# Two-bank score tiles, work placed at the ends of matmul groups, and an earlier load in a fused attention and MLP kernel

## The chip, the cores and the metric

The kernel runs on one core of a Trainium2 chip. The metric is the device time of one execution in microseconds (us). Before the change it was 414.0 us (median of three runs, 413.62 to 414.21). Runs of this kernel scatter by about 1%.

PE is the matmul engine, ACT evaluates activations, DVE is the vector engine, POOL the general-purpose engine, which here also issues the DMA transfers of the "software" queue; SP issues those of a "hardware" queue.

## The reference

```python
# q, k, v: (8, 12, 448, 64); w_in: (768, 2048); w_out: (2048, 768)
scores = q @ k.transpose(0, 1, 3, 2) / sqrt(64)
attn   = maximum(scores, 0) ** 2 / 448
x      = (attn @ v).transpose(0, 2, 1, 3).reshape(3584, 768)
h      = x @ w_in
out    = (maximum(h, 0) ** 2) @ w_out
```

The score part of one batch is three *units* of four heads, and each unit has seven *tiles*. There are 24 units (0 to 23) and 168 tiles in all.

## The kernel before

The program interleaves attention with the two large products. A *visit* computes two score tiles, takes the relu of them on ACT, does the product with v ("av", copied into xt, the transposed x) of two tiles of two visits ago, and squares the new tiles on DVE. Visits stand between the matmuls of h = x w_in (groups of six accumulating matmuls into one PSUM bank) and of the output product (groups of 16).

PSUM has eight banks: two for av, two for h and output ("mm"), four for a score tile pair ("s"). There is one such score slot.

```python
load16(n):  q, k of unit n as fp16, DMA from POOL with a cast (units 0 to 5; PE transposes them)
load_qk(n): q, k of unit n as fp32; cast_qk(n) casts them on POOL,
            dma_transpose(n) transposes them by DMA, issued from SP (units 6 to 23)

def scores(tiles):                      # cut to the part after the first stage
    at = at_p.tile([P, 4, S], FP16, name="at", tag="at")
    ps = slot(FP32)                     # four banks, one slot
    for z, t in enumerate(tiles):
        score(t, ps, z)
    nc.scalar.activation(out=at[:, 0:m], in_=ps[:, 0:m, 0:S], func=AF.Relu, scale=SK)

def enter_unit(n):                      # when the visits reach unit n
    m = n + 2
    if NPE + 2 <= m + 1 < NUN:
        load_qk(m + 1, nc.sync)
    if NPE <= m < NUN:                  # NPE = 6
        cast_qk(m)
        load_v(m)
        dma_transpose(m)

    ...                                 # loads issued from POOL, at the sixth visit
    load16(5); load_w1(3); load_v(5)
    for z in range(4):
        load_w2(z)                      # w_out, 768 KB each
    load_qk(6, nc.gpsimd)
    load_qk(7, nc.gpsimd)
    ...
    for cost, fn in steps:              # every h or output matmul is one step
        while ev and ev[0][0] <= clock: # visits may fall before any step
            ...
        fn()
        clock += cost
```

## Time and profile before

| | before |
|---|---|
| time, median | 414.0 us |
| span of the profiled run | 411.3 us |
| PE busy | 390.4 us (95%) |
| ACT busy | 233.3 us (57%) |
| DVE busy | 171.6 us (42%) |

These lines of the page give the busy time of each engine, and in 40 slices of the span the busy tenths of PE and the clock granted to it in tenths.

```profile
span 411.3 us, 7394 instructions
...
PE 390.4 (95%) x3188; PEld 196.9 (48%) x3188; DVE 171.6 (42%) x196; ACT 233.3 (57%) x283; POOL 79.4 (19%) x94
...
PE   6778996999999999999999999999999999999995
...
PEclk9999998999999999999999999999999999999999
```

PE is the limit nearly everywhere. What a reordering can win is its idle time, 20.9 us, and the time at a lowered clock. The view of waits names what ended PE's idle time: the waiting engine and line, the releaser, then the total in us, the count and the longest.

```profile
PE sps L213 <- DMA kT<-ks: 2.8, 1, 2.8
...
PE hps L321 <- ACT g L329: 1.9, 7, 0.4
...
PE hps L321 <- ACT at L230: 1.1, 1, 1.1
PE sps L213 <- DVE kT L184: 1.0, 2, 0.5
```

The largest single wait is for kT, the transposed k, of unit 6. The timeline of PE around it (start, duration, what, count, and in brackets the idle time before and its releaser):

```profile
63.08 0.93 PE L321 MATMUL hps<-xt,w 128*128 128x448 f16 x4
66.85 0.96 PE L213 MATMUL sps<-qT,kT 64*64 64x448 f16 x8 [2.85 <-DMA kT<-ks]
67.75 3.01 PE L321 MATMUL hps<-xt,w 128*128 128x448 f16 x9
71.01 1.67 PE L321 MATMUL hps<-xt,w 128*128 128x448 f16 x8 [0.25 <-ACT g L329]
```

Nine h matmuls took 3.01 us, where eight take 1.67 a little later: after the wait PE ran at half the clock (granted clock 0.50 from 66.7 to 70.1 us). The chain of waits, in order of time, leads from this wait back to the loads:

```profile
37.81 20.82 DMA qf<-in_q_dram
...
58.69 1.19 POOL qs L109
...
60.15 0.93 POOL ks L109
61.08 0.68 POOL vt L95
...
61.99 4.82 DMA kT<-ks
...
66.85 0.96 PE sps L213 x8
```

q of unit 6 was issued at 37.81 us, behind the four w_out loads of the same queue. Then came POOL's casts and the DMA transpose of k, which took 4.82 us from issue to landing.

### The profile page before, as it was taken

The page shows a single profiled execution, that of the slowest core. Times are in us where ns is not written, and L with a number is a line of the kernel's source. Part 1 is how long each engine was busy: PE and PEld are TensorE (multiplying, and loading weights), DVE is VectorE, ACT ScalarE, POOL GpSimd, SP SyncE. Part 2 cuts the span into 40 slices and gives each one's busy share as a digit, 9 for nine tenths or more (in the row PEclk, how much of TensorE's full clock was granted, in tenths as well). Part 3 has the DMA queues.
Part 4 walks back from the last instruction along what each step waited for, and adds up shares of the span by engine and source line. Part 5 has one row for each costly group of instructions (what it writes and reads, how often), then busy time and mean ns, then how long its engine had stood idle before and what let it go on. Part 6 is the DMA issues. An engine that isn't in the chain of part 4 may idle for free.

```text
span 411.3 us, 7394 instructions
## 1 busy us (share of the span) xinstructions
PE 390.4 (95%) x3188; PEld 196.9 (48%) x3188; DVE 171.6 (42%) x196; ACT 233.3 (57%) x283; POOL 79.4 (19%) x94
## 2 busy tenths in 40 slices
PE   6778996999999999999999999999999999999995
PEld 3333442445555544445555544444555544555663
DVE  1874674553343365563342356573332345220000
ACT  4976783774645567766544666765554575441111
POOL 8534124530020233030022033030000000000000
PEclk9999998999999999999999999999999999999999
DMA  8999999984566797352399776253251210001233
GB/s 126 202 201 206 210 260 204 276 167 81 163 109 164 144 233 163 59 121 47 79 194 209 171 178 156 37 134 55 48 115 47 70 40 0 2 0 40 77 78 77
DMA packets 62496, 50.81 MB, mean 124 GB/s; under 512 B 35712, under 2 KB 58688, under 8 KB 62464
## 3 DMA queue, kind: packets, MB, share of 16 engines
q1 hardware_dynamic: 46752, 33.86, 35.0%
q0 software_dynamic: 15552, 16.39, 24.2%
q8 instruction: 25, 0.41, 0.4%
q10 hardware_dynamic: 160, 0.10, 0.1%
q14 instruction: 7, 0.06, 0.0%
HBM read 45.61 MB, written 11.01 MB: 138 GB/s over the span
## 4 chain that ended last, share of the span: by engine, by line
PE 79%; DMA 14%; ACT 4%; POOL 2%; issue 1%; DVE 0%; POOLq 0%
PE ops L362 36%; PE hps L321 29%; PE sps L213 8%; PE avt L254 5%; DMA qf<-in_q_dram 5%; DMA w<-in_moe_w_in_dram 3%; ACT at L224 3%; DMA k<-in_k_dram 2%; DMA q<-in_q_dram 2%; DMA kT<-ks 1%; ACT g L329 1%; POOL vt L95 0%; POOL k L90 0%; POOL qs L109 0%; POOL q L89 0%
## 5 line engine op out<-in xcount | busy, mean ns | idle before, releaser
L321 PE MATMUL hps<-xt,w 128*128 128x448 f16 x768 | 156.7, 355 | 4.0 <-ACT g L329 1.9
L224 ACT ACTIVATE at<-sps 128x1792 f16<-128x1792 f32 x73 | 121.5, 1664 | 63.6 <-PE sps L213 63.4
L240 DVE TENSOR_TENSOR at<-at 128x1792 f16<-128x1792 f16 (+1 forms) x95 | 95.0, 1013 | 140.5 <-ACT at L224 137.5
L362 PE MATMUL ops<-w,g 128*128 128x384 f16 x896 | 152.0, 326 | 0.2 <-ACT g L329 0.2
L362 PEld LDWEIGHTS <-g 128*128 128x128 f16 x896 | 85.0, 98 | 66.1 <-issue 12.3
L321 PEld LDWEIGHTS <-w 128*128 128x128 f16 x768 | 71.6, 98 | 84.3 <-issue 24.3
L329 ACT ACTIVATE g<-hps 128x448 f16<-128x448 f32 x128 | 68.5, 543 | 49.8 <-PE hps L321 49.6
L332 DVE TENSOR_TENSOR g<-g 128x896 f16<-128x896 f16 x64 | 47.7, 746 | 32.0 <-ACT g L329 31.4
L384 ACT ACTIVATE osb<-ops 128x384 f32<-128x384 f32 x55 | 27.0, 490 | 49.5 <-PE ops L362 45.6
L109 POOL CAST qs<-qf 128x896 f16<-128x896 f32 x18 | 20.7, 1148 | 173.8 <-DMA qf<-in_q_dram 137.0
L254 PE MATMUL avt<-at,vt 64*64 64x448 f16 x672 | 46.9, 350 | 2.6 <-DVE xt L268 2.4
L213 PE MATMUL sps<-qT,kT 64*64 64x448 f16 x584 | 42.2, 364 | 5.0 <-DMA kT<-ks 2.8
L268 DVE TENSOR_SCALAR xt<-avt 128x896 f16<-128x896 f32 x23 | 25.0, 1087 | 18.8 <-PE avt L254 18.7
L213 PEld LDWEIGHTS <-kT 64*64 64x64 f16 x672 | 14.1, 105 | 35.9 <-issue 27.0
L254 PEld LDWEIGHTS <-vt 64*64 64x64 f16 x672 | 19.8, 107 | 16.0 <-issue 5.7
L109 POOL CAST ks<-kf 128x896 f16<-128x896 f32 x18 | 22.1, 1229 | 3.9 <-POOL qs L109 2.0
L230 ACT ACTIVATE at<-slot 128x896 f16<-128x896 f32 x22 | 18.5, 924 | 1.3 <-PE slot L213 1.1
L95 POOL DMA_DIRECT2D vt<-in_v_dram x24 | 17.3, 720 | 2.3 <-DMA w<-in_moe_w_in_dram 1.2
L378 DVE TENSOR_SCALAR osb<-ops 128x192 f32<-128x192 f32 x1 | 0.4, 358 | 35.6 <-ACT osb L375 35.6
L213 PE MATMUL slot<-qT,kT 64*64 64x448 f16 x88 | 7.2, 358 | 2.0 <-ACT kT L182 0.7
L132 POOL DMA_DIRECT2D w<-in_moe_w_in_dram x8 | 5.3, 666 | 3.4 <-DMA w<-in_moe_w_in_dram 1.2
L171 PE MATMUL slot<-zeros 128*128 128x448 f16 x12 | 4.6, 542 | 1.2 <-DVE zeros L147 1.2
(29 smaller groups left out, 40.7 us busy)
## 6 DMA issues: line engine op xcount, KB each, us to landing
out_dram<-osb SPq DMA_DIRECT2D x54, 192.0 KB, 2.7
qf<-in_q_dram SPq DMA_DIRECT2D x16, 448.0 KB, 5.0
kf<-in_k_dram SPq DMA_DIRECT2D x16, 448.0 KB, 5.6
vt<-in_v_dram POOLq DMA_DIRECT2D x24, 224.0 KB, 4.8
w<-in_moe_w_in_dram POOLq DMA_DIRECT2D x8, 384.0 KB, 11.7
w<-in_moe_w_out_dram POOLq DMA_DIRECT2D x4, 768.0 KB, 16.7
q<-in_q_dram POOLq DMA_DIRECT2D x6, 224.0 KB, 7.8
k<-in_k_dram POOLq DMA_DIRECT2D x6, 224.0 KB, 8.3
```

The costliest lines, as they stand in the source:

```text
L109: nc.gpsimd.tensor_copy(t.rearrange("p j h d -> p h j d"), src.rearrange("p h (j d) -> p h j d", d=D))
L213: nc.tensor.matmul(ps[c, 2 * z + hh, 0:S], lhsT=kT[r, j, c], rhs=qT[r, :, c], start=True, stop=True)
L224: nc.scalar.activation(out=at[:, 0:m], in_=ps[:, 0:m, 0:S], func=AF.Relu, scale=SK)
L230: nc.scalar.activation(out=at[:, 2 * z:2 * z + 2], in_=ps[:, :, 0:S], func=AF.Relu, scale=SK)
L240: nc.vector.tensor_mul(at[:, a:a + step], at[:, a:a + step], at[:, a:a + step])
L254: nc.tensor.matmul(ap[64 * hh:64 * hh + 64, hp, 0:S], lhsT=vt[r, hh, j * D:(j + 1) * D], rhs=at[r, hh, :], start=(j == 0), stop=(j == J - 1))
L268: nc.vector.tensor_scalar(out=xts[b][:, 2 * u:2 * u + 2, :], in0=ap[:, :, 0:S], scalar1=CX, scalar2=None, op0=ALU.mult)
L321: nc.tensor.matmul(cell[f][:, 0:S], lhsT=w1[f // 4][:, m, (f % 4) * P:(f % 4 + 1) * P], rhs=xts[b][:, m, :], start=(m == 0), stop=(m == NM ...
L329: nc.scalar.activation(out=g[:, f % 2], in_=cell[f][:, 0:S], func=AF.Relu)
L332: nc.vector.tensor_mul(g, g, g)
L362: nc.tensor.matmul(cell[0][:, 0:HALF], lhsT=gts[pr][f // 2][:, f % 2, tb * P:(tb + 1) * P], rhs=w2[f // 4][:, f % 4, hf * HALF:(hf + 1) * ...
L384: nc.scalar.activation(out=cell[1][:, z:z + HALF], in_=cell[0][:, 0:HALF], func=AF.Copy, scale=CO)
```

## The change

Its intent was to take these waits away:

- Score tiles of two PSUM banks in two slots, each with its own relu and square, instead of one slot of four banks.
- Among the h matmuls, visits and PE transposes only before the first matmul of a group (with one exception in batch 1); among the output matmuls they may stand anywhere, as before. The transposes of units 4 and 5 stand two groups ahead of their use.
- q and k of unit 6 are loaded ahead of w_out.
- In batch 0 every second h relu goes to DVE. The first h groups take the banks of a third score slot, which the first stage uses alone. The first visit to unit 6 comes eight h matmuls later than before.
- Smaller parts: v of unit 6 is loaded earlier, and the last copy of x for batch 1 is split between ACT and DVE, as that of batch 0 already was.

```diff
-    slot_p = first.enter_context(tc.tile_pool(name="slots", bufs=3, space=PSUM))
+    s_p = ctx.enter_context(tc.tile_pool(name="sps", bufs=2, space=PSUM))
+    third_p = first.enter_context(tc.tile_pool(name="third", bufs=1, space=PSUM))
 ...
+        ps = slot(FP32)                  # two banks, now inside score(t)
 ...
+        at = at_p.tile([P, 2, S], FP16, name="at", tag="at")
+        nc.scalar.activation(out=at, in_=ps[:, :, 0:S], func=AF.Relu, scale=SK)
 ...
+        for t in ready:
+            nc.vector.tensor_mul(ats[t], ats[t], ats[t])
 ...
+        return [(0.1892, step(m), m == 0 or (b == 1 and f == 0 and m == 4))
+                for m in range(NM)]
 ...
-            for z in range(4):
-                load_w2(z)
             load_qk(6, nc.gpsimd)
-            load_qk(7, nc.gpsimd)
+    load_v(6)
+    for z in range(4):
+        load_w2(z)
+    load_qk(7, nc.gpsimd)
 ...
-        while ev and ev[0][0] <= clock:
+        while ev and edge and ev[0][0] <= clock + 1e-3:
```

The number of matmuls, of visits and of transferred bytes stays the same.

More of the change, by code (lines that the diff above doesn't have):

```diff
@@ L63 @@
     v_p = ctx.enter_context(tc.tile_pool(name="vp", bufs=6))
-    at_p = ctx.enter_context(tc.tile_pool(name="atp", bufs=6))
+    at_p = ctx.enter_context(tc.tile_pool(name="atp", bufs=12))
     x_p = ctx.enter_context(tc.tile_pool(name="xp", bufs=3))
@@ L159 @@
     big: dict = {}
+    slot_no = [0]
     def slot(dtype):
-        if "s" in big:
-            return big["s"].tile([P, 4, 2048 // mybir.dt.size(dtype)], dtype,
-                                 name="sps", tag="s")
-        return slot_p.tile([P, 2, 2048 // mybir.dt.size(dtype)], dtype,
-                           name="slot", tag="slot")
+        slot_no[0] += 1
+        third = "mm" not in big and slot_no[0] % 3 == 2
+        return (third_p if third else s_p).tile(
+            [P, 2, 2048 // mybir.dt.size(dtype)], dtype, name="slot", tag="slot")
     def warm(n):
@@ L204, with score @@
     ats: dict = {}
-    def score(t, ps, z):
+    seen: dict = {}
+    now = [0]
+    av_order: deque = deque(range(NUN * J))
+    avt = [None]
+    def score(t):
         n, j = divmod(t, J)
         qT, kT = qkt[n]
+        ps = slot(FP32)
         for hh in range(2):
@@ L213, in score @@
                 nc.tensor.matmul(
-                    ps[c, 2 * z + hh, 0:S], lhsT=kT[r, j, c], rhs=qT[r, :, c],
+                    ps[c, hh, 0:S], lhsT=kT[r, j, c], rhs=qT[r, :, c],
                     start=True, stop=True)
-    def scores(tiles):
-        at = at_p.tile([P, 4, S], FP16, name="at", tag="at")
-        if "s" in big:
-            m = 2 * len(tiles)
-            ps = slot(FP32)
-            for z, t in enumerate(tiles):
-                score(t, ps, z)
-            nc.scalar.activation(
-                out=at[:, 0:m], in_=ps[:, 0:m, 0:S], func=AF.Relu, scale=SK)
-        else:
-            for z, t in enumerate(tiles):
-                ps = slot(FP32)
-                score(t, ps, 0)
-                nc.scalar.activation(
-                    out=at[:, 2 * z:2 * z + 2], in_=ps[:, :, 0:S], func=AF.Relu,
-                    scale=SK)
-        for z, t in enumerate(tiles):
-            ats[t] = at[:, 2 * z:2 * z + 2]
-        return at
-    def square(at, m):
-        step = 2 * m if "s" in big else 2
-        for a in range(0, 2 * m, step):
-            nc.vector.tensor_mul(at[:, a:a + step], at[:, a:a + step], at[:, a:a + step])
-    avt = [None]
+        at = at_p.tile([P, 2, S], FP16, name="at", tag="at")
+        nc.scalar.activation(out=at, in_=ps[:, :, 0:S], func=AF.Relu, scale=SK)
+        ats[t] = at
+        seen[t] = now[0]
     def av_round(t):
@@ L260, in av_round @@
                 xts[b] = x_p.tile([P, NM, S], FP16, name="xt", tag="xt")
-            if n == 2:
-                nc.scalar.activation(out=xts[b][:, 4, :], in_=ap[:, 0, 0:S],
+            xt = xts[b]
+            if b < 2 and u == NU - 1:
+                nc.scalar.activation(out=xt[:, 4, :], in_=ap[:, 0, 0:S],
                                      func=AF.Copy, scale=CX)
                 nc.vector.tensor_scalar(
-                    out=xts[b][:, 5, :], in0=ap[:, 1, 0:S],
+                    out=xt[:, 5, :], in0=ap[:, 1, 0:S],
                     scalar1=CX, scalar2=None, op0=ALU.mult)
@@ L268, in av_round, with av_some @@
                 nc.vector.tensor_scalar(
-                    out=xts[b][:, 2 * u:2 * u + 2, :], in0=ap[:, :, 0:S],
+                    out=xt[:, 2 * u:2 * u + 2, :], in0=ap[:, :, 0:S],
                     scalar1=CX, scalar2=None, op0=ALU.mult)
-    av_queue: deque = deque()
-    def av_some(upto, most):
+    def av_some(lag=2, most=3):
         done = 0
-        while av_queue and av_queue[0] <= upto and done < most:
-            t = av_queue.popleft()
+        while av_order and done < most:
+            t = av_order[0]
+            if t not in seen or seen[t] > now[0] - lag:
+                break
+            av_order.popleft()
             av_round(t)
@@ L281, in av_some, with prefetch, visit @@
                 break
-    seen = [0]
-    def enter_unit(n):
-        m = n + 2
+    def prefetch(m):
+        if m >= NUN:
+            return
         if NPE + 2 <= m + 1 < NUN:
             load_qk(m + 1, nc.sync)
-        if NPE <= m < NUN:
-            cast_qk(m)
+        cast_qk(m)
+        if m > NPE:
             load_v(m)
-            dma_transpose(m)
-    def visit(tiles, upto, most=3, turn=None):
+        dma_transpose(m)
+    def visit(tiles, turn=None, lag=2, most=3):
+        now[0] += 1
@@ L295, in visit @@
         for t in tiles:
-            if t % J == 0 and t >= 3 * J:
-                enter_unit(t // J)
-        at = scores(tiles) if tiles else None
+            if t % J == 0 and t >= (NPE - 2) * J:
+                prefetch(t // J + 2)
+        for t in tiles:
+            score(t)
         if turn is not None:
             pe_transpose(turn)
-        av_some(upto, most)
-        if tiles:
-            square(at, len(tiles))
-        av_queue.extend(tiles)
+        ready = list(tiles)
+        av_some(lag, most)
@@ L307, with h_group, step @@
+        for t in ready:
+            nc.vector.tensor_mul(ats[t], ats[t], ats[t])
     gts: dict = {}
-    def h_steps(b):
+    def h_group(b, f):
         pr = b // 2
-        if b % 2 == 0:
-            gts[pr] = []
         z = (b % 2) * S
-        steps = []
-        cell: dict = {}
-        def step(f, m):
+        cell = [None]
+        def step(m):
             def run():
                 if m == 0:
-                    cell[f] = big["mm"].tile([P, 512], FP32, name="hps", tag="mm")
+                    cell[0] = big["mm"].tile([P, 512], FP32, name="hps", tag="mm")
@@ L321, in run @@
                 nc.tensor.matmul(
-                    cell[f][:, 0:S],
+                    cell[0][:, 0:S],
                     lhsT=w1[f // 4][:, m, (f % 4) * P:(f % 4 + 1) * P],
                     rhs=xts[b][:, m, :], start=(m == 0), stop=(m == NM - 1))
-                if m == NM - 1:
-                    if b % 2 == 0 and f % 2 == 0:
-                        gts[pr].append(g_p.tile([P, 2, 2 * S], FP16, name="g", tag="g"))
-                    g = gts[pr][f // 2][:, :, z:z + S]
+                if m < NM - 1:
+                    return
@@ L329, in run @@
+                gs = gts.setdefault(pr, [])
+                if len(gs) <= f // 2:
+                    gs.append(g_p.tile([P, 2, 2 * S], FP16, name="g", tag="g"))
+                g = gs[f // 2][:, :, z:z + S]
+                if b == 0 and f % 2 == 1:
+                    nc.vector.tensor_scalar(
+                        out=g[:, f % 2], in0=cell[0][:, 0:S],
+                        scalar1=0.0, scalar2=None, op0=ALU.max)
+                else:
                     nc.scalar.activation(
-                        out=g[:, f % 2], in_=cell[f][:, 0:S], func=AF.Relu)
@@ L331, in run @@
-                    if f % 2 == 1:
-                        nc.vector.tensor_mul(g, g, g)
-            return run
-        order = [(f, m) for f in range(NF) for m in range(NM)]
-        if b < 2:
-            order.sort(key=lambda fm: (fm[0] // 2, fm[1] >= 4, fm)
-                       if fm[0] < 2 else (fm[0] // 2, 0, fm))
-        for f, m in order:
-            steps.append((0.1892, step(f, m)))
-        return steps
+                        out=g[:, f % 2], in_=cell[0][:, 0:S], func=AF.Relu)
@@ L343, in store @@
+                if f % 2 == 1:
+                    nc.vector.tensor_mul(g, g, g)
+            return run
+        return [(0.1892, step(m), m == 0 or (b == 1 and f == 0 and m == 4))
+                for m in range(NM)]
     def store(pr, tb, osb, c, eng):
@@ L395, in o_steps @@
                 for f in range(NF):
-                    steps.append((0.1625, step(tb, hf, f)))
+                    steps.append((0.1625, step(tb, hf, f), True))
         return steps
+    NB0 = NU * J
     warm(10)
     pe_transpose(0)
-    NB0 = NU * J
     for i in range(11):
-        visit([2 * i, 2 * i + 1], 2 * (i - 2) + 1, turn={1: 1, 4: 2, 7: 3}.get(i))
+        visit([2 * i, 2 * i + 1], turn={1: 1, 4: 2, 7: 3}.get(i))
         if i == 0:
@@ L417 @@
             load_v(5)
-            for z in range(4):
-                load_w2(z)
             load_qk(6, nc.gpsimd)
-            load_qk(7, nc.gpsimd)
+    load_v(6)
+    for z in range(4):
+        load_w2(z)
+    load_qk(7, nc.gpsimd)
     first.close()
-    for nm, n in (("mm", 2), ("s", 1)):
-        big[nm] = ctx.enter_context(tc.tile_pool(name=nm + "ps", bufs=n, space=PSUM))
-    events = []
-    T_H = NF * NM * 0.1892
+    big["mm"] = ctx.enter_context(tc.tile_pool(name="mmps", bufs=2, space=PSUM))
+    f0, f1 = h_group(0, 0), h_group(0, 1)
+    front = f0[0:4] + f1[0:4]
+    for _, fn, _ in front:
+        fn()
+    av_some(0, 9)
+    visit([NB0 + 1, NB0 + 2])
+    T_G = NM * 0.1892
+    T_H = NF * T_G
     T_O = NT_PAIR * 2 * NF * 0.1625
     T_P = 2 * T_H + T_O
-    seq = [11, 12, -4, 13, 14, 15, -5, 16, 17, 18, 19, 20]
-    events.append((1.5, [], NB0 - 1))
-    for z, i in enumerate(seq):
-        at = 2.0 + z * (T_H - 5.0) / 11
-        if i < 0:
-            events.append((at, None, -i))
-        else:
-            events.append((at, [2 * i, 2 * i + 1], 2 * (i - 2) + 1))
-    events.append((T_H - 1.6, [], 39))
-    events.append((T_H - 0.3, [], 41))
-    at0 = T_H + 0.5
-    for pr in range(1, 4):
+    events = []
+    seq = [[3, 4], 4, [5, 6], [7, 8], [9, 10], 5, [11, 12], [13, 14], [15, 16],
+           [17, 18], [19, 20], [], []]
+    for i, ts in enumerate(seq):
+        at = (2 + i) * T_G
+        if isinstance(ts, int):
+            events.append((at, lambda n=ts: pe_transpose(n)))
+        else:
+            events.append((at, lambda ts=ts: visit([NB0 + t for t in ts])))
+    events.append((T_H + 7 * 0.1892, lambda: av_some(0, 9)))
+    at0 = T_H + 2 * T_G
+    for pr in range(1, B // 2):
         t0 = 2 * NB0 * pr
@@ L447 @@
         for i in range(21):
-            t = t0 + 2 * i
-            events.append((at0 + i * gap, [t, t + 1], t - 3))
+            ts = [t0 + 2 * i, t0 + 2 * i + 1]
+            events.append((at0 + i * gap, lambda ts=ts: visit(ts)))
         at0 = end
     for i in range(3):
-        events.append((at0 + 0.3 + i, [], NUN * J))
-    steps = []
-    for pr in range(B // 2):
-        steps += h_steps(2 * pr) + h_steps(2 * pr + 1) + o_steps(pr)
-    clock = 0.0
-    ev = deque(events)
-    for cost, fn in steps:
-        while ev and ev[0][0] <= clock:
-            _, tiles, upto = ev.popleft()
-            if tiles is None:
-                pe_transpose(upto)
-            else:
-                visit(tiles, upto)
-        fn()
+        events.append((at0 + 0.3 + i, lambda: visit([])))
+    steps = [(0.1892, None, False)] * 8 + f0[4:] + f1[4:]
+    for f in range(2, NF):
+        steps += h_group(0, f)
+    f0, f1 = h_group(1, 0), h_group(1, 1)
+    steps += f0[0:4] + f1[0:4] + f0[4:] + f1[4:]
+    for f in range(2, NF):
+        steps += h_group(1, f)
+    steps += o_steps(0)
+    for pr in range(1, B // 2):
+        for b in (2 * pr, 2 * pr + 1):
+            for f in range(NF):
+                steps += h_group(b, f)
+        steps += o_steps(pr)
+    clock = 0.0
+    ev = deque(sorted(events, key=lambda e: e[0]))
+    for cost, fn, edge in steps:
+        while ev and edge and ev[0][0] <= clock + 1e-3:
+            ev.popleft()[1]()
+        if fn is not None:
+            fn()
         clock += cost
+    assert not ev and not av_order
 _INS = ['q', 'k', 'v', 'moe_w_in', 'moe_w_out']
```

## The prediction

> **What bounds it now.** The page's table of engines has PE busy 390.4 of 411.3 us; ACT is at 57%, DVE 42%, POOL 19%. So only PE's 20.9 us of idle time, and matmuls run at a lowered clock, can be won. The PE timeline and the PE waits place the idle time:
> - 0 to 27 us: about 6.9 us. Here ACT evacuates scores back to back (9.51 of 10 us busy in 10 to 20).
> - 27 to 62 us: 1.1 us (first h matmul waits for the last early relu, whose PSUM it takes over), 0.9 (xt of batch 0), 0.5 (score slot), 1.0 (kT copies after the transposes).
> - 64.0 to 66.85 us: 2.85 us for kT of unit 6. The chain of waits leads back to the load of its q, issued at 37.8 us behind four w_out loads and landed near 58. After this wait the windows show a granted clock of 0.50 (68 to 70 us); 9 h matmuls took 3.0 us instead of 1.7, a score visit 0.96 instead of 0.57: 1.7 us more. The Trainium skill, "TensorE: Matmul & The Clock Gate", section "What's actually happening", gives half the clock after an idle window of about 3.4 us, which fits.
> - 71 us on: about 1.9 us, eight waits of an h (or first out) matmul for its PSUM bank, whose relu stood behind a 1.66 us score relu.
> - The end: 4.4 us.
>
> **What the change does.**
> - Score relu: 73 of 128x1792 (1664 ns) become 146 of 128x896 (924 ns each; 846 apart back to back). That is 184 ns more per visit, 13 us of ACT busy time, as the skill's page "ScalarE: Activation LUTs", "What ACT_TABLE_LOAD costs", has it (186 ns + 0.833 per element; the trace agrees). Squares likewise: 2 x 548 for about 1010 ns. Neither engine bounds after 62 us, so this costs nothing there. In batch 0's h stage it is tight: per two visits about 4.0 us of ACT and 4.0 of DVE (odd relus go to DVE) against 4.3 of PE. I charge up to 1 us.
> - Two slots of two banks: transposes no longer take the only slot, and stand two groups ahead of use: minus 1.5 us.
> - h takes over the third slot's banks, free two relus earlier: minus 1 us; a score visit fills the xt wait: minus 0.5.
> - Visits at group edges: the preceding h relu is ahead of the score relus, so the bank is free in time: minus 1.5 us.
> - Unit 6 ahead of w_out: its q and k should land near 46 us, kT near 55. PE reaches it near 62. Minus 2.85 and 1.7 us.
> - Visits, matmuls and mode switches stay the same in number: PE work unchanged.
>
> Sum about -9.5 us, nearly all on PE, which is the critical path.
>
> **Prediction:** 404.5 us, range 401.5 to 408.5. Faster by over 2%: 0.66; within 2%: 0.32; slower: 0.02.
>
> **Right if:** PE idle falls to about 12 us; no wait for kT by DMA; granted clock near 1.00 from 60 to 70 us; PE's waits for the h relu nearly gone; ACT busy rises to about 240 us; the first out matmuls start near 83 to 84 us instead of 92. PE's time from there to the end shrinks by only about 1 us.
>
> **Wrong if:** unit 7's q and k, now last behind w_out and competing with unit 8's load (which starts earlier), land so late that kT of unit 7 (I estimate 71 us, needed near 75) stalls PE instead: up to 4 us back. Or ACT and DVE, both over 90% in batch 0's h stage, fall behind, so that av matmuls or h banks wait there: 1 to 3 us back. Or the early stage, bound by ACT, does not hand over sooner.

## The result, and the profile after

The changed kernel took 406.76 us (median of four runs, 406.32 to 408.73) against 413.81 us. The ratio was 0.9844, 95% interval 0.9805 to 0.9884: 1.6% faster, inside the predicted range, but not clear of 2%. A ratio here is always the mean time of one kernel's fast runs over that of the other's in the same rounds, so it is not quite the ratio of the medians.

```profile
span 404.6 us, 7633 instructions
...
PE 388.8 (96%) x3188; PEld 196.3 (49%) x3188; DVE 184.2 (46%) x277; ACT 233.9 (58%) x349; POOL 74.3 (18%) x94
...
PE   7689799999999999999999999999999999999995
...
PEclk9999899999999999999999999999999999999999
```

PE's idle time fell by 5.1 us to 15.8 us, not to 12. ACT's busy time did not rise to 240 us. The slow slice of PE and of its clock has moved forward, from about 60 to 70 us to about 40 to 50. PE's waits, changed kernel:

```profile
PE slot L219 <- DVE kT L185: 2.9, 2, 2.5
...
PE slot L219 <- DMA kT<-ks: 0.7, 1, 0.7
...
PE hps L304 <- ACT at L223: 0.3, 1, 0.3
```

The waits for the h relu are gone. The wait for kT of unit 6 is down to 0.7 us, but there is a new one of 2.5 us for a kT copy. PE's timeline, changed kernel:

```profile
44.23 0.38 PE L219 MATMUL slot<-qT,kT 64*64 64x448 f16 x4
47.16 0.59 PE L219 MATMUL slot<-qT,kT 64*64 64x448 f16 x4 [2.54 <-DVE kT L185]
47.53 0.96 PE L237 MATMUL avt<-at,vt 64*64 64x448 f16 x8
48.42 2.30 PE L304 MATMUL hps<-xt,w 128*128 128x448 f16 x6
...
61.60 4.83 PE L304 MATMUL hps<-xt,w 128*128 128x448 f16 x24
67.15 0.57 PE L219 MATMUL slot<-qT,kT 64*64 64x448 f16 x8 [0.72 <-DMA kT<-ks]
```

Six h matmuls took 2.30 us at 48.42; at full clock six take 1.31. And PE still cannot start unit 6 before 67.15 us (66.85 before). The chain of waits, changed kernel, says why:

```profile
42.96 3.09 DVE at L290 x2
...
46.16 20.94 DMA kT<-ks
...
67.15 0.57 PE slot L219 x8
```

The load of unit 6 came in early, the casts were done at 45.55 us, and the DMA transpose of k was issued at 46.16. But it took 20.94 us to land, where it took 4.82 before. It now ran beside the w_out loads.

The pair of squares at 42.96 us is slow too: two squares take 1.15 us elsewhere in this stage. These are lines of DVE and POOL from the timeline of all engines, changed kernel:

```profile
42.87 3.16 DVE L290 TENSOR_TENSOR at<-at 128x896 f16<-128x896 f16 x2
...
43.73 0.94 POOL L110 CAST qs<-qf 128x896 f16<-128x896 f32 x1
...
44.61 0.94 POOL L110 CAST ks<-kf 128x896 f16<-128x896 f32 x1
...
45.96 0.61 DVE L185 COPY qT<-slot 128x896 f16<-128x896 f16 x1
```

The first square took 0.62 us, the second 2.63; it ended only after both of POOL's casts. The Trainium skill, "SBUF — State Buffer", section "Who interferes with whom", says that a DVE instruction with two SBUF inputs contends with a POOL instruction that reads SBUF, and that whoever issues first makes the other wait. The amount fits: 2.0 us of delay against 1.82 us of casts. The order does not quite: the trace has the held square start 0.3 us before the first cast, and times on POOL are rough.

### The profile page after: what moved, and what is told of

It reads as the page before. It is cut to its first block, busy times and chain, and to the rows that moved or that the text cites. A ratio compares the mean times of both kernels' runs of the same rounds, so it can differ in the third digit from the quotient of the medians.

```text
span 404.6 us, 7633 instructions
## 1 busy us (share of the span) xinstructions
PE 388.8 (96%) x3188; PEld 196.3 (49%) x3188; DVE 184.2 (46%) x277; ACT 233.9 (58%) x349; POOL 74.3 (18%) x94
## 4 chain that ended last, share of the span: by engine, by line
PE 85%; DMA 7%; DVE 4%; ACT 2%; POOL 1%; issue 1%; SPq 0%; ACTq 0%; POOLq 0%
PE ops L347 37%; PE hps L304 33%; PE slot L219 8%; PE avt L237 6%; DMA kT<-ks 5%; DVE at L290 2%; DMA k<-in_k_dram 2%; ACT at L223 1%; DVE xt L252 1%; PE slot L192 1%; DVE qT L185 0%; POOL q L90 0%; DVE kT L185 0%; POOL k L91 0%; POOL vt L96 0%
## 5 line engine op out<-in xcount | busy, mean ns | idle before, releaser
L223 ACT ACTIVATE at<-slot 128x896 f16<-128x896 f32 x168 | 144.4, 918 | 47.3 <-PE slot L219 45.4
L304 PE MATMUL hps<-xt,w 128*128 128x448 f16 x768 | 155.0, 355 | 0.9 <-ACT at L223 0.3
L290 DVE TENSOR_TENSOR at<-at 128x896 f16<-128x896 f16 x168 | 108.7, 666 | 93.7 <-ACT at L223 93.7
L319 ACT ACTIVATE g<-hps 128x448 f16<-128x448 f32 x120 | 65.3, 545 | 55.0 <-PE hps L304 54.6
L322 DVE TENSOR_TENSOR g<-g 128x896 f16<-128x896 f16 x64 | 43.4, 679 | 52.6 <-ACT g L319 51.8
L219 PE MATMUL slot<-qT,kT 64*64 64x448 f16 x672 | 49.7, 362 | 5.2 <-DVE kT L185 2.9
L110 POOL CAST qs<-qf 128x896 f16<-128x896 f32 x18 | 19.2, 1064 | 168.3 <-DMA qf<-in_q_dram 142.4
L237 PEld LDWEIGHTS <-vt 64*64 64x64 f16 x672 | 19.6, 107 | 15.8 <-issue 5.9
L110 POOL CAST ks<-kf 128x896 f16<-128x896 f32 x18 | 18.7, 1041 | 8.7 <-DMA kf<-in_k_dram 7.2
L185 DVE COPY qT<-slot 128x896 f16<-128x896 f16 x6 | 3.7, 621 | 6.7 <-PE slot L192 6.7
L315 DVE TENSOR_SCALAR g<-hps 128x448 f16<-128x448 f32 x8 | 5.0, 619 | 2.0 <-PE hps L304 2.0
```

The costliest lines, as they stand in the source:

```text
L110: nc.gpsimd.tensor_copy(t.rearrange("p j h d -> p h j d"), src.rearrange("p h (j d) -> p h j d", d=D))
L219: nc.tensor.matmul(ps[c, hh, 0:S], lhsT=kT[r, j, c], rhs=qT[r, :, c], start=True, stop=True)
L223: nc.scalar.activation(out=at, in_=ps[:, :, 0:S], func=AF.Relu, scale=SK)
L237: nc.tensor.matmul(ap[64 * hh:64 * hh + 64, hp, 0:S], lhsT=vt[r, hh, j * D:(j + 1) * D], rhs=at[r, hh, :], start=(j == 0), stop=(j == J - 1))
L290: nc.vector.tensor_mul(ats[t], ats[t], ats[t])
L304: nc.tensor.matmul(cell[0][:, 0:S], lhsT=w1[f // 4][:, m, (f % 4) * P:(f % 4 + 1) * P], rhs=xts[b][:, m, :], start=(m == 0), stop=(m == NM ...
```

## The experiments

My first theory (A) was that the changed kernel has two limits that hide each other: the square held up by the casts, with the half clock after it, and the DMA transpose under w_out. The rivals were the prediction's own view (the load order is worth 4.5 us) and the chain of waits taken at its word (the transfer alone is the limit).

Each time below is the median of five or six runs (four in the first row), and each ratio is to the kernel before in the same rounds. After the first row there are three sets, each on one chip: e1 to e4; c_after, e5, e6 and e8; e7, e9, e10 and e11.

| run | time us | ratio to before | 95% interval | kT of unit 6 landed, us | PE waited for it, us |
|---|---|---|---|---|---|
| changed kernel, first | 406.8 | 0.9844 | 0.9805 to 0.9884 | 67.1 | 0.7 |
| e1_order_undone | 404.9 | 0.9803 | 0.9770 to 0.9836 | 64.4 | 1.1 |
| e2_wout_late | 401.9 | 0.9751 | 0.9713 to 0.9790 | 49.8 | 0 |
| e3_cast_act | 408.1 | 0.9876 | 0.9842 to 0.9910 | 66.2 | 4.1 |
| e4_both | 402.2 | 0.9748 | 0.9718 to 0.9777 | 49.9 | 0 |
| c_after (changed kernel again) | 407.6 | 0.9874 | 0.9835 to 0.9913 | 68.8 | 4.8 |
| e5_before_order | 412.2 | 0.9985 | 0.9948 to 1.0021 | 66.0 | 2.5 |
| e6_mid_group | 408.3 | 0.9898 | 0.9862 to 0.9933 | 66.4 | 4.6 |
| e8_before_wout_late | 411.6 | 0.9966 | 0.9930 to 1.0002 | 51.6 | 0 |
| e9_unit6_on_pe | 405.0 | 0.9814 | 0.9791 to 0.9838 | none needed | 0 |
| e10_half_wout | 402.8 | 0.9762 | 0.9727 to 0.9797 | 58.8 | 0 |
| e11_before_wout_late_act | 410.4 | 0.9950 | 0.9922 to 0.9978 | 52.4 | 0 |
| e7_before_edges | 409.6 | 0.9917 | 0.9892 to 0.9942 | 67.0 | 3.3 |

The landing time is the issue of the transpose of k plus its time to landing, both from the DMA view of that tile.

### The load order undone (changed kernel)

```diff
             load_v(5)
+            for z in range(4):
+                load_w2(z)
             load_qk(6, nc.gpsimd)
+            load_qk(7, nc.gpsimd)
     load_v(6)
-    for z in range(4):
-        load_w2(z)
-    load_qk(7, nc.gpsimd)
```

> The changed kernel with one part undone: w_out is loaded ahead of q and k of unit 6 again. Theory A (two limits that hide each other: in the changed kernel the early cast of unit 6 on POOL slows DVE, so that the kT copy of unit 5 comes 2.5 us late and the clock is halved after it, and unit 6's DMA transpose then waits behind w_out until 67.1 us anyway): the cast moves to about 60 us, the pair of squares near 43 us takes about 1.15 us instead of 3.16, the 2.5 us wait and the half clock at 48 us are gone, and PE comes to unit 6 near 62.5 us and waits 4 to 6 us there. Total within 2 us of the changed kernel: ratio to before 0.980 to 0.989. Theory P (the prediction's: the order alone is worth 2.85 + 1.7 us): 4 to 5 us slower than the changed kernel, ratio about 0.994.

Undoing the early load cost nothing: 404.9 us. The prediction's view is refuted. Theory A had the total about right (the ratio is at the edge of its band), but not the wait, which was 1.10 us instead of 4 to 6. With w_out out of the way the transpose of k, issued at 60.44 us, landed 3.9 us later, at 64.4 us, so *earlier* than in the changed kernel, which had issued it 14 us sooner.

### w_out behind unit 7 (changed kernel)

```diff
     load_v(6)
-    for z in range(4):
-        load_w2(z)
     load_qk(7, nc.gpsimd)
 ...
         dma_transpose(m)
+        if m == NPE + 1:
+            for z in range(4):
+                load_w2(z)
```

> The changed kernel with the four w_out loads moved behind unit 7's q and k and behind unit 7's casts. Theory A: the transposes of unit 6 no longer run under w_out, kT of unit 6 lands by about 53 us instead of 67.1, the 0.72 us wait for it goes; the 2.5 us wait for the kT copy and the half clock near 48 us stay, since the casts still run on POOL near 44 us. Total 0 to 1.5 us below the changed kernel: ratio 0.980 to 0.985. Rival (the chain of waits taken at its word: the 20.9 us of the kT transfer are what bounds): 3 to 4 us below the changed kernel, ratio about 0.975.

The rival was right and theory A was wrong here: 401.9 us, with no wait for kT and no half clock. PE reached unit 6 at 62.27 us and went straight on. SP's timeline for this run (SPq is its queue: start and duration of the issue, not of the transfer):

```profile
45.54 1.63 SPq L122 DMA_TRANSPOSE kT<-ks  x1
...
49.80 1.59 SPq L122 DMA_TRANSPOSE kT<-ks  x1
...
70.62 7.16 SPq L122 DMA_TRANSPOSE kT<-ks  x1
```

And PE's timeline for the same run, where the wait for kT used to be:

```profile
57.50 4.83 PE L307 MATMUL hps<-xt,w 128*128 128x448 f16 x24
62.27 0.57 PE L219 MATMUL slot<-qT,kT 64*64 64x448 f16 x8
```

The transpose at 45.54 us landed after 4.2 us. The next two are those of units 7 and 8; they run under the w_out loads that were moved there. Unit 7's landed after 19.6 us; unit 8's took 7.16 us for its issue alone and landed after 16.2 us. The slow transposes moved with w_out, to a place where PE does not wait for them. The 2.5 us hold-up was absent as well, although POOL made the same casts: DVE's squares started at 42.14 us, ahead of them, and this time the cast was the longer one (1.29 us instead of 0.93).

### Unit 6 cast by ACT, and both edits together (changed kernel)

```diff
+            if n == NPE:
+                nc.scalar.activation(out=o_, in_=i_, func=AF.Copy)
+            else:
+                nc.gpsimd.tensor_copy(o_, i_)
 ...
-            events.append((at, lambda n=ts: pe_transpose(n)))
+            events.append((at, lambda n=ts: (pe_transpose(n), prefetch(NPE) if n == NPE - 1 else None)))
```

> The changed kernel with the casts of unit 6 alone made by ACT instead of POOL, two groups later, right behind the transposes of unit 5; loads as in the changed kernel. Theory A (POOL's casts hold up the DVE squares): the pair of squares near 43 us takes about 1.15 us, the 2.5 us wait for the kT copy and the half clock are gone, PE reaches unit 6 near 62.5 us but its kT still lands at 65 to 67 us, so 3 to 5 us are given back there: total within 1.5 us of the changed kernel, ratio 0.980 to 0.988. Rival (DVE has simply too much work in this stage): the squares still end late and the wait for the kT copy stays above 1.5 us.

> Both edits: unit 6 cast on ACT and w_out loaded behind unit 7. Theory A (the two limits hide each other): neither wait is left, PE reaches unit 6 near 62.5 us and goes on; 3.5 to 5 us below the changed kernel, 402 to 403.5 us, ratio 0.970 to 0.976, far more than the sum of the two edits made alone. If the edits simply add: the sum of what the other two runs show, about 0 to 1.5 us.

With the casts on ACT alone, PE came early (62.2 us) and waited 4.07 us, as theory A said. The half clock came after that wait: 18 h matmuls took 5.26 us instead of 3.6. Total 408.1 us. With both edits it was 402.2 us, in the band of theory A, but no better than w_out late alone. So w_out under the transpose is the limit that had to go. This pair does not say what the hold-up of the square costs, because the profile of w_out late alone had none to take away; the run with half of w_out late, below, had one.

### The changed kernel once more, and the order alone in the kernel before

```diff
+            load_qk(6, nc.gpsimd)
             for z in range(4):
                 load_w2(z)
-            load_qk(6, nc.gpsimd)
             load_qk(7, nc.gpsimd)
```

> The changed kernel itself once more, as the control for this call. Ratio to before 0.981 to 0.988. If PE comes to unit 6 early in this profile (no square held up by POOL's casts), it should wait about 4 us there for kT, as in the run with the casts on ACT; if a square is held up, about 1 us or less: the time comes out the same within 1.5 us either way.

> The kernel before with one part of the change alone: q and k of unit 6 loaded ahead of w_out. Theory A (the transposes of unit 6 then run under w_out's loads and land when those are done): casts near 44 us, transposes issued near 46, kT landed at 63 to 67 us all the same; time within 2 us of before, ratio 0.995 to 1.003. Theory P (the prediction's): the 2.85 us wait and the half clock after it go, 4 to 4.5 us faster, ratio about 0.989.

Both came out as expected. The order alone is worth 0.15%, within noise. The changed kernel again took 407.6 us, and in this profile no square was held up: none fell beside unit 6's casts, only copies did, and they took their usual 0.61 us. Where DVE stands when the casts come differs between runs of the same kernel, so the run with the casts on ACT cannot by itself prove what held the square. PE's timeline for this second profile of the changed kernel:

```profile
59.21 4.83 PE L304 MATMUL hps<-xt,w 128*128 128x448 f16 x24
68.85 0.96 PE L219 MATMUL slot<-qT,kT 64*64 64x448 f16 x8 [4.80 <-DMA kT<-ks]
69.74 5.39 PE L304 MATMUL hps<-xt,w 128*128 128x448 f16 x18
```

And the issue of the transpose, in SP's timeline of the same profile:

```profile
47.67 6.67 SPq L122 DMA_TRANSPOSE kT<-ks  x1
```

The transpose was issued at 47.67 us and landed 21.1 us later. PE waited 4.80 us, and then ran 18 h matmuls in 5.39 us instead of 3.58.

### Visits inside h groups again (changed kernel), and the edges alone (kernel before)

```diff
 # changed kernel: from the second pair of batches on
-        return [(0.1892, step(m), m == 0 or (b == 1 and f == 0 and m == 4))
+        return [(0.1892, step(m), b > 1 or m == 0 or (b == 1 and f == 0 and m == 4))
 # kernel before: from batch 1 on
+            steps.append((0.1892, step(f, m), b == 0 or m == 0))
 ...
+        while ev and edge and ev[0][0] <= clock:
```

> The changed kernel with one part undone: from the second pair of batches on, visits may fall inside an h group again. If the group edge is what removed PE's waits for h banks: 3 to 6 waits of 0.2 to 0.4 us for the h relu come back after 100 us, 1 to 2 us slower than the changed kernel. Rival (the score relu in two halves is what removed them): no such wait over 0.1 us, same time within 0.5 us.

> The kernel before with one part of the change alone: from batch 1 on, visits start only at the first matmul of an h group. If the edge removes the waits for h banks by itself: the 8 waits for the h relu (2.1 us of PE idle after 70 us) are gone, 1.5 to 2.5 us below before, ratio 0.994 to 0.997. If it takes the halved score relu as well: waits of 0.2 to 0.4 us stay, less than 1 us gained.

Undoing the edges made the changed kernel 1.2 us longer from its first output matmul to its end (317.9 us against 316.7), though only one wait of 0.5 us shows. That is the lower end of the expectation; in total time the two ratios (0.9898 and 0.9874) are not apart. Putting the edges alone into the kernel before gained more than expected: 409.6 us, ratio 0.9917. Of eight waits for the h relu one of 0.3 us was left. From the first output matmul to the end it took 316.7 us, against 318.9 before and 316.7 in the changed kernel. So the edges alone make the whole gain of that part. The halved relu adds nothing there once visits are at the edges; where they are not, it seems to soften the loss.

### w_out late in the kernel before

The edit is that of the changed kernel above, in `enter_unit`.

> The kernel before with w_out loaded behind unit 7's q, k and casts, all else as it was. If it is w_out's traffic under the transposes that matters and not the order of unit 6: kT of unit 6 lands by about 53 us, the 2.85 us wait and the half clock after it are gone, 3.5 to 5 us faster than before, ratio 0.988 to 0.992. If the early load is worth nothing in this schedule either: ratio 0.997 to 1.003.

This missed: about 1 us gained, not 3.5 to 5. The wait for kT by DMA did go. But with all four loads of units 6 and 7 early, POOL's four casts ran one after the other in the middle of the busy stage. Lines of DVE and PE from the timeline of all engines, kernel before with w_out late:

```profile
46.11 3.29 DVE L240 TENSOR_TENSOR at<-at 128x1792 f16<-128x1792 f16 x1
...
51.06 0.57 PE L213 MATMUL sps<-qT,kT 64*64 64x448 f16 x8 [3.00 <-DVE kT L184]
```

A square that takes 1.09 us took 3.29 and PE waited 3.00 us for the kT copy behind it. To test that, unit 7's casts went to ACT, with one column of each read by POOL as a gate, so that the w_out loads stay where they were; the call that starts these casts stands behind the transposes of unit 5 now:

```diff
+            if n == NPE + 1:
+                nc.gpsimd.tensor_copy(gate, src[:, 0, 0:1])
+                nc.scalar.activation(out=o_, in_=i_, func=AF.Copy)
+            else:
+                nc.gpsimd.tensor_copy(o_, i_)
 ...
+                if upto == NPE - 1:
+                    enter_unit(NPE - 1)
```

> The kernel before with w_out behind unit 7, as in the earlier run that gained only about 1 us, and now with unit 7's casts made by ACT in its idle time near 46 us (POOL reads one column of each as a gate). If POOL's casts held the DVE square for 2.2 us and so made the 3.0 us wait for the kT copy: that square takes about 1.1 us, the wait falls to about 0.5 us, the time to 2.5 to 4 us below before: ratio 0.990 to 0.994. Rival (DVE is late there for another reason): the wait stays over 2 us, ratio 0.996 or more.

The same two places in the timeline of this run:

```profile
49.11 1.07 DVE L245 TENSOR_TENSOR at<-at 128x1792 f16<-128x1792 f16 x1
...
51.84 0.57 PE L218 MATMUL sps<-qT,kT 64*64 64x448 f16 x8 [0.83 <-DVE kT L189]
```

The square was back at 1.07 us and the wait at 0.83. The time was 410.4 us, ratio 0.9950: the gain is at the lower end of what was expected, and the interval overlaps that of the run above. In this profile the first h matmul started 2.9 us later than in that one (30.24 against 27.30 us), because an early k load came in late. From the first h matmul to the end it took 379.7 us, against 382.2 there and 383.7 in the kernel before. The rival is refuted by the trace; the size of the gain in time is less sure.

### Unit 6 transposed by PE, and half of w_out late (changed kernel)

```diff
 # e9
-        if m >= NUN:
+        if m >= NUN or m == NPE:
 ...
-            load_qk(6, nc.gpsimd)
+            load16(6)
 ...
-           [17, 18], [19, 20], [], []]
+           [17, 18], [19, 20], 6, [], []]
 # e10
-    for z in range(4):
+    for z in range(2):
         load_w2(z)
 ...
+        if m == NPE + 1:
+            for z in range(2, 4):
+                load_w2(z)
```

> The changed kernel, loads in the same order, but unit 6 is loaded as fp16 and transposed by PE (as units 0 to 5 are), so it needs neither POOL's casts nor a DMA transpose. Theory A (the load of unit 6 is early enough; it is its DMA transpose that waits for w_out's queue): no wait for kT of unit 6, PE comes to it near 63 us with 0.9 us of transposes added; 2.5 to 4.5 us below the changed kernel, 402.5 to 404.5, ratio 0.976 to 0.981. Rival (the loads themselves come too late, the transpose only passes it on): a wait of some us for the q or k load of unit 6 near 56 to 60 us, no gain.

> The changed kernel with two of the four w_out loads moved behind unit 7. If the landing of unit 6's kT follows the end of the software queue's backlog: it lands at 56 to 60 us (67 to 69 with all four ahead, about 50 with none), before PE needs it near 62; no wait, time as with all four moved: ratio 0.974 to 0.979. Rival (a transpose under any w_out load takes about 20 us): landed at 65 us or later, a wait of 3 us or more, ratio as the changed kernel's.

With unit 6 transposed by PE and w_out ahead as in the change, no wait for unit 6 was left, neither for a load nor for kT; 405.0 us, just outside the expected band. The interval of its ratio overlaps those of both measurements of the changed kernel, but from the first h matmul to the end it took 374.1 us, against 377.4 and 380.2 in the two profiles of the changed kernel. So the loads were early enough, and the DMA transpose was what came late. With two of the four w_out loads moved, the transpose landed after 13.4 us, at 58.8 us, and the time was 402.8 us. So the delay grows with the amount of w_out ahead: 4.2 us with none, 13.4 with two loads, 19.6 to 21.1 with all four, in five profiles that had them all ahead (the changed kernel twice, two variants of it, and the kernel before with the order alone). In these five and in the half-w_out run, kT landed within about 1 us of the last load that then stood in the software queue, k of unit 7 (66.9 and 67.1 us in the changed kernel, 57.8 and 58.8 with half of w_out late). But the transpose does not always wait for that queue to run empty: with all of w_out late in the changed kernel, unit 7's kT landed at 69.4 us, while two of the four w_out loads landed after it, at 75.8 and 81.0 us.

The half-w_out run also had casts of POOL beside squares again (the two squares near 43 us took 1.20 and 1.35 us), and PE waited for a kT copy. Its view of waits:

```profile
PE slot L219 <- DVE kT L185: 2.2, 2, 1.8
```

No half clock followed. From the first h matmul to the end it took 374.8 us, against 373.3 with all of w_out late and 373.4 with both edits, where there was no such wait. So the hold-up can be a second, smaller limit once kT is in time; no run isolates what it is worth.

## Why the prediction was right or wrong, point by point

**The step that failed** reads: "Unit 6 ahead of w_out: its q and k should land near 46 us, kT near 55. PE reaches it near 62. Minus 2.85 and 1.7 us." The first part held: POOL cast q at 43.73 us. The second did not: kT landed at 67.1 and 68.8 us. I had costed the transpose with about the 4.8 us that it took in the trace of before, where the software queue had nearly run empty. The change moved it to a place where w_out was queued. The Trainium skill, "DMA: Bandwidth & Descriptors", section "Queues, rings and completion order", says that every DMA engine takes turns among its queues, so I should have asked whether the loads would slow the transpose. The traces here show the slower transpose, not the turns. Instead of 4.55 us the order was worth about nothing: ratio 0.9985 alone in the kernel before, and 404.9 against 406.8 and 407.6 us when taken out of the changed kernel, so if anything it is a loss there (other rounds, and the intervals touch).

The measured time fell inside the range all the same, and that was partly luck: of the 9.5 us predicted, these 4.55 did not come, but the edges gave about 1.9 us more than predicted, and the range was wide enough for the rest.

**The terms of the sum:**

| term | predicted us | measured us | how |
|---|---|---|---|
| h takes over the third slot's banks | -1.0 | -0.8 | wait 1.13 before, 0.33 after |
| two slots, earlier transposes, xt wait filled, less up to 1 for a tight stage | -2.0 to -1.0 | about -2.3 | read from the trace, not isolated: from the first h matmul to the twelfth of batch 1, waits for unit 6 left out, 38.0 us before (27.51 to 64.0 plus 8 x 0.189), 35.7 in the second profile of the changed kernel (28.39 to 64.05) |
| visits at group edges | -1.5 | about -3.4 | ratio 0.9917 with this alone in the kernel before |
| unit 6 ahead of w_out | -4.55 | about 0 | ratio 0.9985 alone |

**Why 3 us of front gain are not all in the time.** PE's first two terms bring it to unit 6 earlier, but kT lands at 64 to 69 us whatever the load order, as it did before (66.8 us). What is left of them is that PE does eight more h matmuls (1.5 us) before it has to stop. With 3.4 us from the edges this makes about 4.9 us, and the second measurement of the changed kernel gave 5.1 us. The first gave 7.05 us. A cause for that can be argued from its profile, but no run isolates it: there the square was held up, so the stop and the half clock fell at 44 to 50 us, in time that PE would have spent waiting for kT anyway, and after a wait of only 0.7 us the clock stayed up. In the second profile the half clock came after the wait and cost 2.2 us (0.96 for 0.57 and 5.39 for 3.58).

**What to see in the profile.** The waits for the h relu are gone: right. No wait for kT by DMA: wrong, 0.7 and 4.8 us. Clock near 1.00 from 60 to 70 us: true in the first profile only because the half clock had moved to 47 to 50 us; in the second it was half from 66.6 to 73.5 us. ACT busy 240 us: wrong, 233.9. I had added 184 ns per visit to the engine's busy time, but two halves run back to back overlap, 1.72 us a pair against 1.66 for the whole, and eight h relus went to DVE. First output matmul at 83 to 84 us: wrong, 87.9 and 91.8; with w_out late it is 83.06, so the rest of the estimate holds once the failed step is made good. From there to the end about 1 us: wrong, 2.2 us (318.9 to 316.7). The waits for the h relu show there as only 1.4 us of idle time in the kernel before (1.2 for h, 0.2 for output matmuls), so that view understated what they cost: PE's busy time in that part fell as well, from 313.4 to 312.4 us, with the same matmuls.

**What could go wrong.** I had named unit 7's k as the one that might come late behind w_out. The same thing happened, to unit 6. I had named DVE as tight in batch 0's stage. It did fall behind in one profile of two, not by its own work but by POOL's casts.

**What stays open.** How the w_out loads slow a DMA transpose was not tested. Nor was the two-slot part run alone.

A version that beats both kernels came out of this: the change with w_out behind unit 7, 401.9 us (ratio 0.9751).

## What to carry to other kernels

When a transfer is made to start earlier, ask what will share the DMA engines with it *then*: a duration read from the old trace belongs to the old traffic. An early start does not help a step whose successor then runs beside a large transfer; move the large transfer that is needed late, not the small one that is needed soon. Let a visit stand where an accumulation group ends, so that the relu that frees its bank is queued ahead of the visit's own long relus.

## What the Trainium skill lacked or had wrong

- "DMA: Bandwidth & Descriptors", section "DMA Transpose (X-bar)", gives no time for a DMA transpose beside a busy software queue. Here that of unit 6's k took 3.9 to 6.4 us with no w_out load left ahead in that queue, 13.4 us with two of them (768 KB each) and 19.6 to 21.1 us with four.
- "TensorE: Matmul & The Clock Gate", sections "What's actually happening" and "Why this matters for your kernels", gives an idle window of about 3.4 us and a rule of no gaps over about 3 us. Here gaps of 2.48 us (the order alone in the kernel before), 2.54 us (changed kernel) and 2.85 us (kernel before) were followed by half the clock, and one of 3.00 us (w_out late in the kernel before) was not. The page calls the window free-running, but does not say how busy PE may be in a window that counts as idle. In these traces the clock changes at whole multiples of 3.41 us (in the changed kernel 40.96 us full, 3.41 half, 354.99 full). In the 3.41 us just before the half clock PE was busy for 0.97 us (changed kernel) and 0.93 us (order alone). The gap of 3.00 us fell across two such stretches, with 1.50 and 2.32 us busy.
- "SBUF — State Buffer", section "Who interferes with whom", describes a lock for one instruction. Here one square waited for two casts that followed each other, 2.63 us instead of 0.62. The trace has that square start 0.3 us before the casts, so by the page's rule it should have gone first, unless the rough times of POOL mislead here.
- "Perfetto Trace Analysis" warns that matmul ends are estimated, but gives no size for it. Here waits that show as 1.4 us of idle time after the first output matmul were worth 2.2 us (318.9 against 316.7) when they were removed; that the estimated ends are the reason was not tested.
